# Zeros on TensorE ahead of the first operands, and two early transfers issued by ScalarE

## The chip, the cores and the metric

The kernel runs on one core of a Trainium2 chip. The core has five engines that run their own instruction streams and wait for each other by semaphores: TensorE (PE; its weight loads are listed apart as PEld), VectorE (DVE), ScalarE (ACT), GpSimd (POOL) and SyncE (SP), which here issues nearly all transfers. The transfers themselves run on 16 DMA engines. The metric is the device time of one execution in microseconds; the median of several runs is compared.

## The reference

Two layers on separate inputs, put side by side: attention with 32 heads of 32, and a real-valued Fourier mixing written as products with cosine and sine matrices.

```python
def _A_ref(x, wqkv, wo):                      # x [1, 2048, 1024]
    qkv = ((x @ wqkv).reshape(B, S, 3, 32, 32)).transpose(2, 0, 3, 1, 4)
    q, k, v = qkv[0], qkv[1], qkv[2]
    p = _softmax(jnp.einsum("bhqd,bhkd->bhqk", q, k) * scale, axis=-1)
    o = jnp.einsum("bhqk,bhkd->bhqd", p, v)
    return o.transpose(0, 2, 1, 3).reshape(B, S, D) @ wo

def _B_ref(x, dft_seq_re, dft_seq_im, dft_hid_re, dft_hid_im):
    a = jnp.einsum("bsd,ed->bse", x, dft_hid_re)
    b = jnp.einsum("bsd,ed->bse", x, dft_hid_im)
    return jnp.einsum("ts,bse->bte", dft_seq_re, a) - jnp.einsum("ts,bse->bte", dft_seq_im, b)

out = jnp.concatenate([A_ref(...), B_ref(...)], axis=-1)
```

## The kernel before

The large products are done in Strassen's manner: seven products of sums and differences of blocks in place of eight. Every float32 operand is split in two parts that TensorE takes in one pass each: a rounded high part and the remainder, the low part. A product of two operands is three matmuls: high by high, low by high, high by low. In the trace the high part is a CAST on DVE or an ACTIVATE on ACT (line 442 or 440, in `halves`), the low part a subtraction on DVE or POOL (line 445).

The stage that the change touches is the first one, `qkv`, which makes queries, keys and values. Its first step (`STEPS`, line 549) loads a piece of the query weights, W0, and four tiles of x of 128x512 (`load_x(0, k)`, k from 0 to 3), then runs the first group of twelve matmuls (`group`, line 346; the matmul is line 356): four chunks, three matmuls each, W0 against x0 to x3. The next group takes the second piece of weights, W1, against the same tiles; then come groups with tiles x4 to x7, and then groups with the value weights wv. The results are stored to DRAM (`qk_d`) and loaded again in another layout as `qs` and `ks` for the attention, whose first score matmul is line 1147.

A load is made in `fetch` (line 382): one operand is one transfer of 256 KB, issued on line 404; where a step needs a sum or difference of blocks, a second transfer (line 413) and an addition (line 420) follow. In this stage first operands go to a ring of ten buffers, named `er`, and second operands to a ring of five, named `raw`. A ring is taken in order, and a transfer may start when those who used its buffer before are done.

The program order of all engines is written out by a planner (`Plan`): while the kernel is built it plays the whole of it through with assumed durations. Each operation has an engine, a cost, and some have a second engine that can take it (`other`): the high part may go to DVE or ACT, the low part to POOL or DVE. At each step of its clock the planner goes through ACT, DVE, POOL and SP in this order, and gives a free engine the lowest-ranked operation whose inputs are there (`others`, `choose`). DVE's copies and subtractions share a port with POOL, so the planner runs them one at a time. PE's order has three attention streams (scores S, transposed scores T, values V) and a list of fills, which are the matmuls of all dense products in fixed order; which goes next depends on the planner's clock. On the chip each engine then works through its list strictly in that order.

For a transfer the planner takes 360 KB a microsecond on one pipe, plus 1.6 us to land. When one engine's result is used on another, 0.1 us is added (0.2 after PE), and for some pairs of engines a slack on top:

```python
    LAT = 0.1
    LAT_PE = 0.2
    SLACK = {("SP", "POOL"): 2.0, ("SP", "DVE"): 2.0, ("SP", "PE"): 2.0, ("POOL", "DVE"): 0.7}
    KB_US = 360.0
    LANDING = 1.6
    QUEUE = 1.0
```

The key of the slack is the engine that ran the first operation and the first-named engine of the second. The high part's first-named engine is DVE, the low part's POOL. SP issues its next transfer in the plan no earlier than 1.0 us (`QUEUE`) before the pipe is free; this rule is for SP alone (`begin`, line 204).

PSUM banks for dense products come from two pools of two, `psT` and `psD` (tile `pd`); the first group uses `psT`, the second `pd`.

Of the kernel before, what the change touches and what calls it, by code (L numbers as in the profile page):

```python
# [8 lines left out]
F32 = mybir.dt.float32  # L9
F32R = mybir.dt.float32r  # L10
# [6 lines left out]
P = 128  # L17
# [6 lines left out]
NB = 512  # L24
NPT = 19
NE = 4
PVB = 4
PAIRS = 3
NV = 4
SCALE = float(DH) ** -0.5  # L30
# [30 lines left out]
class Plan:  # L61
# [23 lines left out]
    def op(self, engine, cost, emit, after=(), uses=(), rank=0.0, kb=0, order=None, other=None, lanes=1, two=False):  # L85

        o = Op(engine, cost, emit, rank, kb, other, two)
        o.lanes = lanes  # L90
        seen = set()
        for d in after:
            if d is not None and id(d) not in seen:
                seen.add(id(d))
                self._wait(o, d)
        for u in uses:
            u.append(o)
        if order is not None:
            p, order.first = order.first, o
            if p is not None and not p.begun:  # L100
                p.soon.append(o)
                o.left += 1
        if o.left == 0:
            self._release(o)
        return o
# [104 lines left out]
def kernel(  # L210
# [11 lines left out]
    nc = tc.nc  # L222

    dram = ctx.enter_context(tc.tile_pool(name="dram", bufs=1, space=DRAM))
    const = ctx.enter_context(tc.tile_pool(name="const", bufs=1))
# [21 lines left out]
    def f(ap):  # L247
        return ap.bitcast(F32)
# [19 lines left out]
    qk0 = tc.alloc_tile_pool(name="qk0", bufs=1)  # L268
    QS, KS = [qk0.tile([98, S], F32R, name="qs0")], [qk0.tile([98, S], F32R, name="ks0")]
    nc.gpsimd.memset(f(KS[0])[96:98, :], 1.0)  # L270
    rec = const.tile([P, 2 * NS], F32, name="rec")
    nc.gpsimd.memset(rec, 1.0)

# [14 lines left out]
    psS, psT, psD = (pools[n] for n in ("psS", "psT", "psD"))  # L288
# [19 lines left out]
    ISSUE = 0.46  # L308
# [11 lines left out]
    ADD = 0.68  # L320
    FILL = 3 * (7 * 24 * 4 + 7 * 16 * 4 + 7 * 8 * 16 + 2 * 8 * 4)
    ATT = H * (128 * MM + 16 * PV + 16 / PVB * SWITCH)

    pl = Plan()
    op = pl.op
# [50 lines left out]
    class Kept:  # L376


        def __init__(self, get):
            self.get, self.made, self.users = get, None, []  # L380

    def fetch(shape, terms, store=None, keep=None):

        box = {}
        raws, seconds, tile_of, gate = where[0]
        rank = seq()
        sign, *first = terms[0]
        loaded = len(first) == 2
        if len(terms) == 1 and not loaded:
            return first[0].get, first[0].made, first[0].users  # L390
        if keep is None:
            old, users = raws.take()
        else:

            old, users = gate + keep.users, keep.users

        def dest():
            if "r" not in box:
                box["r"] = tile_of(shape, "raw", len(raws.users)) if keep is None else keep.get()
            return box["r"]  # L400

        last = None
        if loaded:
            last = op("SP", ISSUE, lambda: nc.sync.dma_start(dest(), first[0]), old + first[1] + gate, [users], rank, 256, raws if keep is None else None)
            old = []
        for sign, *term in terms[1:]:
            other = {}
            if len(term) == 2:
                gold, gusers = seconds.take()

                def load(src=term[0], other=other):
                    other["q"] = tile_of(shape, "g", len(seconds.users))
                    nc.sync.dma_start(other["q"], src)

                q = op("SP", ISSUE, load, gold + term[1] + gate, [gusers], rank, 256, seconds)
            else:
                other["k"], q, gusers = term[0], term[0].made, term[0].users

            def add(e, sign=sign, other=other, a=None if last is not None else first[0]):
                (nc.gpsimd if e == "POOL" else nc.vector).tensor_tensor(  # L420
                    out=dest(), in0=dest() if a is None else a.get(), in1=other["q"] if "q" in other else other["k"].get(), op=ALU.add if sign > 0 else ALU.subtract)

            last = op("POOL", SUB, add, old + [first[0].made if last is None else last, q], [users, gusers] + ([first[0].users] if last is None else []),
                      rank, 0, raws if keep is None and last is None else None, other=("DVE", ADD, 20 + rank), two=True)
            old = []
        if keep is not None:
            keep.made = last
        if store is not None:
            store[1].append(op("SP", ISSUE, lambda: nc.sync.dma_start(store[0], dest()), [last], [users], rank, 256))
        return dest, last, users  # L430
# [103 lines left out]
    def qkv():  # L534
# [31 lines left out]
        def load_x(x, k):  # L566
            where[0] = ahead if x < 5 else within
            p = STEPS[x][0]
            XS[x, k] = moving(8 * ((x + 1) % 2) + k, x_terms(p, k, x >= 5), (tx_d[k], tx[k]) if x == 3 else (t1x_d[k], t1x[k]) if x == 2 else None)
# [176 lines left out]
        def qk_group(x, W, b, n):  # L746
            p = STEPS[x][0]
            early = x < 5
            h = FIRST.get(p)
            if p == 1 and n == 0:  # L750
                if early:
                    X[2 * b], X[2 * b + 1] = acc(b)
                else:
                    X[2 * b], X[2 * b + 1] = accs(16 + b - PAIRS)
            group(((chunk(W, c), (XS[x, 4 * n + c], whole)) for c in range(4)), 4,
                  gather(p, 2 * b + n, qk_result(b + 8 * h[0], 2 * h[1] + n, early) if h else None, early, None if b % 2 else SCALE))
# [8 lines left out]
        for x, (p, blocks, v) in enumerate(STEPS[:10]):  # L765
            spare[0] = x < 5
            for i, b in enumerate(blocks):
                where[0] = ahead if x < 5 else within
                W = piece(w_terms(p, lambda i, j: wqk[b + 8 * i][:, 4 * j : 4 * j + 4, :], sq_d[b], sq[b]), (sq_d[b], sq[b]) if p == 6 else None)
                if x == i == 0:  # L770
                    first = W
                    for k in range(4):
                        load_x(0, k)
                    qk_group(x, W, 0, 0)
                    continue
                if x == 0 and i == 1:
                    for k in range(4, 8):
                        load_x(0, k)
                qk_group(x, W, b, 0)
                if x == 0 and i == 1:  # L780
                    qk_group(x, first, 0, 1)
                qk_group(x, W, b, 1)
                if x == 0:
                    if i == 1:
                        for c in range(4):
                            load_v_weight(0, c)
                else:
                    for k in range(8 * i // len(blocks), 8 * (i + 1) // len(blocks)):
                        load_x(x + 1, k)
            for t in range(8 if v else 0):  # L790
                if p == 1 and t % 2 == 0:
                    X[16 + t], X[17 + t] = acc(PAIRS + t // 2)
                v_group(x, t)
                if x == 0:
                    load_x(1, t)
                if t < 4 and x < 4:
                    load_v_weight(x + 1, t)
            where[0] = within
            if x == 4:
                for u in ahead[0].users:  # L800
                    att_gate.extend(u)
            if x == 9:
                for c in range(4):
                    load_v_weight(10, c)
# [446 lines left out]
    def transposed(h):  # L1251
# [4 lines left out]
        for t in range(NS):  # L1256
            for j in range(4):
# [17 lines left out]
                todo.append((t, j, box, e, puse))  # L1275
            if (t + 1) % PVB == 0:
                load, vuse = vts[h]

                def pv(todo=todo, t=t):
                    po["p"] = psD.tile([P, NB], F32, name="pd")  # L1280
                    for k, j, box, _, _ in todo:
                        nc.tensor.matmul(  # L1282
                            po["p"][j * DH : j * DH + DH, :], VT[h][:, k, :], box["t"], start=(k == t + 1 - PVB), stop=(k == t),
                            tile_position=(0, j * DH),
                        )

                v = op("PE", SWITCH + PVB * PV, pv, [load, *(x[3] for x in todo)], [vuse, *(x[4] for x in todo)])
                todo = []

                def gather_o(t=t):  # L1290
                    if t + 1 == PVB:
                        po["o"] = att().tile([P, NB], F32, name="ot", bufs=2)
# [3 lines left out]

                e = op("DVE", EVAC, gather_o, [v] + (oold if t + 1 == PVB else []), [ouse], -1)
                streams["V"].append((v, h, e))
# [42 lines left out]
    while nf < len(fills) or any(place[n] < len(s) for n, s in streams.items()):  # L1341
# [18 lines left out]
        for n, (o, h, k) in heads.items():  # L1360
# [14 lines left out]
            rank = {"V": 0, "T": 1, "S": 0.5 if stock > SFIRST else 1.5}[n]  # L1375
            if n == "S" and "T" in heads and heads["T"][0].left == 0:
# [4 lines left out]
                if lead > 0:  # L1381
                    rank = 2
            ok.append((rank, n))
        fill = None
        if nf < len(fills):
            o, first, left = fills[nf]
# [64 lines left out]
```

## Time and profile before

| what | us |
|---|---|
| median of 3 runs (3045.86 to 3047.76) | 3046.23 |
| the profiled execution | 3044.43 |
| its span, first to last instruction | 3042.6 |
| PE busy in the span | 3009.5 |
| start of the first matmul | 6.10 |
| start of the first score matmul | 72.32 |

A row of the chain or of the timeline has start, duration, engine, line, operation, what is written from what, and a count; in brackets stands how long the engine was idle before and what released it. SPq marks the issue of a transfer by SP, not its flight. A row of waits has: who waited for whom, microseconds in total, times, the longest. A row of windows has the stretch, its length, the busy time of PE, PEld, DVE, ACT and POOL with counts, the granted clock of TensorE as a share of full speed, the busy share of the DMA engines, and GB/s.

### The profile page before, as it was taken

How to read it: one execution, taken by the hardware profiler on the slowest of the kernel's cores; microseconds unless marked ns; L12 is line 12 of the kernel's file. 1: busy time of each engine (PE TensorE's matmuls, PEld its weight loads, DVE VectorE, ACT ScalarE, POOL GpSimd, SP SyncE). 2: the span in 40 equal slices, each digit the busy share in tenths (PEclk: the TensorE clock that was granted, in tenths of full speed). 3: DMA queues.
4: the chain of work that ended last, by engine and by line, in shares of the span. 5: the costliest groups of instructions: out<-in, count | busy, mean ns of one | idle time of the engine just before them, and what ended most of it. 6: DMA issues, size and time to landing. Idle time of an engine off the chain costs nothing.

```text
span 3042.6 us, 45257 instructions
## 1 busy us (share of the span) xinstructions
PE 3009.5 (99%) x14912; PEld 2145.0 (70%) x14912; DVE 2434.8 (80%) x3284; ACT 2298.1 (76%) x4328; POOL 812.6 (27%) x606
## 2 busy tenths in 40 slices
PE   8999999999999999999999999999999999999999
PEld 7887666676676666667766666666677666666887
DVE  7779888778878887787778888888787788887886
ACT  4347888888888888888888888888888788874321
POOL 2313334222412321220111344232111234331232
PEclk9999999999999999999999999999999999999999
DMA  9975567656735544463434675545433567546942
GB/s 336 348 234 186 187 188 234 216 199 227 232 97 175 174 122 157 147 191 113 149 114 129 201 229 185 149 151 182 128 115 100 147 207 237 168 133 222 376 148 98
DMA packets 374777, 557.53 MB, mean 183 GB/s; under 512 B 109424, under 2 KB 109424, under 8 KB 374544
## 3 DMA queue, kind: packets, MB, share of 16 engines
q1 hardware_dynamic: 374544, 554.64, 56.9%
q8 instruction: 120, 1.97, 0.3%
q14 instruction: 113, 0.93, 0.1%
HBM read 401.41 MB, written 152.57 MB: 182 GB/s over the span
## 4 chain that ended last, share of the span: by engine, by line
PE 89%; DVE 5%; DMA 3%; issue 1%; ACT 1%; SPq 0%; POOL 0%; ACTq 0%; DVEq 0%; POOLq 0%
PE pd L356 38%; PE psT L1264 15%; PE psS L1147 15%; PE pd L1282 14%; PE psT L356 7%; DVE negm L1153 2%; ACT psS L1156 1%; DVE slot L442 0%; DVE h L442 0%; DMA raw<-in_wd 0%; DMA raw<-in_ct 0%; DVE raw L420 0%; DMA qk_d<-e 0%; DMA raw<-in_xa 0%; DVE slot L445 0%
## 5 line engine op out<-in xcount | busy, mean ns | idle before, releaser
L1268 ACT ACTIVATE pt<-psT 128x512 f32<-128x512 f32 x2048 | 1169.0, 638 | 350.4 <-PE psT L1264 336.6
L1153 DVE TENSOR_REDUCE negm<-psS 128x1 f32<-128x1024 f32 x1024 | 1237.7, 1220 | 192.5 <-PE psS L1147 187.0
L1156 ACT ACTIVATE psS<-psS,negm 128x1024 f32<-128x1024 f32 x1024 | 1159.8, 1133 | 91.1 <-DVE negm L1153 87.0
L356 PE MATMUL pd<-slot,h 128*128 128x512 f32 x3304 | 1135.6, 394 | 0.0
L1264 PE MATMUL psT<-qs,ks 98*128 98x512 f32 x2048 | 819.3, 403 | 0.8 <-ACT pt L1268 0.8
L356 PEld LDWEIGHTS pd<-slot,h 128*128 128x128 f32 x3304 | 625.2, 189 | 142.5 <-issue 3.4
L356 PE MATMUL pd<-slot,l 128*128 128x512 f32 x1652 | 651.2, 394 | 0.0
L1264 PEld LDWEIGHTS psT<-qs,ks 98*128 98x128 f32 x2048 | 384.2, 189 | 202.3 <-issue 84.7
L1147 PE MATMUL psS<-ks,qs 96*128 96x512 f32 x1552 | 478.2, 397 | 17.6 <-ACT psS L1156 14.5
L1282 PE MATMUL pd<-pt,vt 128*32 128x512 f32 x4096 | 467.5, 597 | 1.5 <-DVE e L641 1.2
L445 POOL TENSOR_TENSOR l<-raw,h 128x512 fp32r<-128x512 f32 x160 | 214.3, 1340 | 944.7 <-DVE h L442 335.0
L420 POOL TENSOR_TENSOR raw<-raw,g 128x512 f32<-128x512 f32 x197 | 260.2, 1325 | 486.4 <-DMA raw<-in_ct 69.8
L356 PEld LDWEIGHTS pd<-slot,l 128*128 128x128 f32 x1652 | 312.9, 189 | 70.0 <-issue 0.8
L1147 PEld LDWEIGHTS psS<-ks,qs 96*128 96x128 f32 x1552 | 290.2, 189 | 92.7 <-ACT psS L1156 27.5
L1282 PEld LDWEIGHTS pd<-pt,vt 128*32 128x32 f32 x4096 | 120.2, 110 | 277.0 <-issue 256.6
L445 POOL TENSOR_TENSOR slot<-raw,slot 128x512 fp32r<-128x512 f32 x135 | 190.7, 1420 | 389.3 <-DVE slot L442 277.5
L1156 ACT ACTIVATION_READ_ACCUMULATOR psS<-psS,negm 128x1 f32 x1024 | 256.6, 251 | 0.0
L1295 DVE TENSOR_TENSOR ot<-ot,pd 128x512 f32<-128x512 f32 x96 | 65.9, 687 | 166.9 <-PE pd L1282 166.9
L356 PE MATMUL pd<-slot,slot 128*128 128x512 f32 x768 | 194.4, 392 | 0.0
L356 PEld LDWEIGHTS pd<-slot,slot 128*128 128x128 f32 x768 | 144.3, 188 | 32.2 <-DVE slot L442 0.3
L1147 PE MATMUL psS<-ks,qx 96*128 96x512 f32 x496 | 151.8, 397 | 2.8 <-ACT psS L1156 2.5
L442 DVE CAST h<-raw 128x512 fp32r<-128x512 f32 x305 | 141.9, 467 | 13.7 <-PE pd L356 12.0
(117 smaller groups left out, 1986.5 us busy)
## 6 DMA issues: line engine op xcount, KB each, us to landing
raw<-in_ct SPq DMA_DIRECT2D x224, 256.0 KB
g<-in_ct SPq DMA_DIRECT2D x128, 256.0 KB
qk_d<-e SPq DMA_DIRECT2D x52, 512.0 KB
qs<-qk_d SPq DMA_DIRECT2D x128, 192.0 KB
ks<-qk_d SPq DMA_DIRECT2D x128, 192.0 KB
raw<-ab_d SPq DMA_DIRECT2D x96, 256.0 KB
c<-u_d SPq DMA_DIRECT2D x88, 256.0 KB
g<-ab_d SPq DMA_DIRECT2D x80, 256.0 KB
```

Of the source, the lines that this page charges most:

```text
L356: nc.tensor.matmul(box["ps"], a[1]((a[0].hi, a[0].lo)[u]()), b[1]((b[0].hi, b[0].lo)[v]()), start=k == 0, stop=k == n - 1)
L420: (nc.gpsimd if e == "POOL" else nc.vector).tensor_tensor(out=dest(), in0=dest() if a is None else a.get(), in1=other["q"] if "q" in other ...
L442: nc.vector.tensor_copy(hi(), raw())
L445: (nc.gpsimd if e == "POOL" else nc.vector).tensor_tensor(out=lo(), in0=raw(), in1=f(hi()), op=ALU.subtract)
L1147: nc.tensor.matmul(p[:, i * NB : i * NB + NB], (qx["t"] if own else QS[h % 2][0:96])[:, qt * P : qt * P + P], KS[h % 2][0:96, c * 1024 + i ...
L1153: nc.vector.tensor_reduce(out=ST["negm"][:, c, qt : qt + 1], in_=box["p"], axis=AX.X, op=ALU.max, negate=True)
L1156: nc.scalar.activation(box["p"], box["p"], AF.Exp, bias=ST["negm"][:, c, qt : qt + 1], accum_out=ST["sums"][:, c, qt : qt + 1])
L1264: nc.tensor.matmul(box["p"], KS[h % 2][0:98, t * P : t * P + P], QS[h % 2][0:98, j * NB : j * NB + NB], start=True, stop=True)
L1268: nc.scalar.activation(box["t"], box["p"], AF.Exp)
L1282: nc.tensor.matmul(po["p"][j * DH : j * DH + DH, :], VT[h][:, k, :], box["t"], start=(k == t + 1 - PVB), stop=(k == t), tile_position=(0, ...
L1295: nc.vector.tensor_tensor(out=po["o"], in0=po["o"], in1=po["p"], op=ALU.add)
```

## The change

A tile of zeros, 128x128, is set by DVE at the start, and TensorE runs 36 matmuls of it by itself into a bank of `psD`, ahead of everything that the planner orders. The result is not used. The planner does not know of these matmuls. The other part: of the first four tiles of x, the first and third (k = 0 and 2) are issued by ACT's queue instead of SP's, and are operations of engine ACT in the plan too.

```diff
+WARM = 36
...
+    zeros = const.tile([P, P], F32R, name="zeros")
+    nc.vector.memset(f(zeros), 0.0)
...
+    ps = psD.tile([P, NB], F32, name="pd")
+    for k in range(WARM):
+        nc.tensor.matmul(ps[:, 0:P], zeros, zeros, start=True, stop=True)
+
     pl = Plan()
...
+    queue = ["SP"]
...
-            last = op("SP", ISSUE, lambda: nc.sync.dma_start(dest(), first[0]), old + first[1] + gate, [users], rank, 256, raws if keep is None else None)
+            q = queue[0]
+            last = op(q, ISSUE, lambda: (nc.scalar if q == "ACT" else nc.sync).dma_start(dest(), first[0]), old + first[1] + gate, [users], rank, 256, raws if keep is None else None)
...
                     for k in range(4):
+                        queue[0] = "SP" if k % 2 else "ACT"
                         load_x(0, k)
+                    queue[0] = "SP"
```

## The prediction

> **What bounds the kernel now.** I read the page's busy times first, then PE's waits over the whole span, then the first 12 us in order of time, then windows of the first 80 us.
>
> ```profile
> span 3042.6 us, 45257 instructions
> PE 3009.5 (99%) x14912; PEld 2145.0 (70%) x14912; DVE 2434.8 (80%) x3284; ACT 2298.1 (76%) x4328; POOL 812.6 (27%) x606
> ...
> DMA  9975567656735544463434675545433567546942
> ...
> PE psS L1147 <- ACT psS L1156: 17.0, 19, 4.0
> PE psS L1147 <- DMA ks<-qk_d: 2.6, 1, 2.6
> ```
>
> TensorE is the bound: 33.1 us of the span are not PE-busy. Of these 6.1 are the wait for the first operand (next rows), 2.6 a wait for the first keys of the attention, 17.0 waits in the attention for ScalarE to free a score bank; the rest is small. So all that the change can touch by its own words is the 6.1 us and how fast the matmuls run right after.
>
> ```profile
> 0.73 1.28 ACT L440 ACT_TABLE_LOAD   x1 [0.73 <-PEq L1444]
> 0.74 0.39 SPq L404 DMA_DIRECT2D er<-in_wqk  x1
> 1.19 1.83 SPq L404 DMA_DIRECT2D er<-in_xa  x4
> 3.32 0.63 ACT L440 ACTIVATE h<-er 128x512 fp32r<-128x512 f32 x1 [1.31 <-DMA er<-in_wqk]
> 3.99 0.69 DVE L445 TENSOR_TENSOR l<-er,h 128x512 fp32r<-128x512 f32 x1 [3.99 <-ACT h L440]
> 5.41 1.32 ACT L440 ACTIVATE slot<-er 128x512 fp32r<-128x512 f32 x2 [1.46 <-DMA er<-in_xa]
> 6.10 0.79 PE L356 MATMUL psT<-slot,h 128*128 128x512 f32 x1 [6.10 <-ACT slot L440]
> 6.16 3.21 SPq L404 DMA_DIRECT2D er<-in_wv  x4
> 7.31 0.63 ACT L440 ACTIVATE slot<-er 128x512 fp32r<-128x512 f32 x1 [0.57 <-DMA er<-in_xa]
> 9.67 0.69 DVE L445 TENSOR_TENSOR l<-er,h 128x512 fp32r<-128x512 f32 x1
> 10.53 0.63 PE L356 MATMUL psT<-slot,l 128*128 128x512 f32 x1
> 10.95 0.43 DVE L442 CAST slot<-er 128x512 fp32r<-128x512 f32 x1
> 10.96 0.63 PE L356 MATMUL psT<-slot,h 128*128 128x512 f32 x1
> 11.38 0.44 PE L356 MATMUL pd<-slot,h 128*128 128x512 f32 x1
> 11.63 0.33 SPq L413 DMA_DIRECT2D raw<-in_xa  x1
> 11.66 0.39 PE L356 MATMUL pd<-slot,l 128*128 128x512 f32 x1
> 11.89 0.39 PE L356 MATMUL pd<-slot,h 128*128 128x512 f32 x1
> ...
> 6.10 5.50 PE psT L356 x12
> ```
>
> The first tile of x lands at 5.41 and is rounded by ScalarE; the first matmul starts at 6.10. Starts then come 0.43 us apart (10.53, 10.96, 11.38) until about 11.5 and 0.23 apart from there (11.66, 11.89). The twelve matmuls of the first group (last row, from the chain of waits) start between 6.10 and the next group's 11.38, 5.28 us; at 0.228 they would take 2.74. **The slow clock costs 2.54 us** here. The windows print a granted clock of 1.00 for this stretch, so the clock must be read from the spacing until the first change is recorded.
>
> ```profile
> 0.00:10.00 10.00, 3.90 (x9) 3.09 (x10) 3.75 (x6) 5.44 (x8) 2.13 (x6) 1.00 0.73 237
> 10.00:20.00 10.00, 10.00 (x41) 7.81 (x40) 8.61 (x12) 7.36 (x14) 2.73 (x2) 1.00 1.01 364
> 60.00:70.00 10.00, 10.00 (x46) 8.29 (x45) 8.40 (x13) 3.79 (x6) 3.03 (x2) 1.00 0.99 350
> ...
> 76.00:77.00 1.00, 1.00 (x5) 0.81 (x4) 1.00 (x2) 0.39 (x1) 0.00 (x0) 0.67 0.54 100
> 77.00:78.00 1.00, 1.00 (x3) 0.73 (x3) 1.00 (x2) 1.00 (x2) 0.68 (x1) 0.50 0.86 266
> 79.00:80.00 1.00, 1.00 (x5) 0.76 (x4) 0.89 (x1) 0.95 (x2) 1.00 (x1) 0.63 1.02 404
> ...
> 75.29 0.96 PE L1147 MATMUL psS<-ks,qs 96*128 96x512 f32 x3 [2.58 <-DMA ks<-qk_d]
> ```
>
> From 10 us on the transfers are full (DMA share 0.96 to 1.02, the column before the last, in every 10 us up to 70), and at 72.7 TensorE runs into them: 2.58 us for keys. The clock then falls to 0.50 for about 3.4 us (0.66 + 2 + 0.74, from the shares of the rows at 76, 77 to 79 and 79), worth 1.7 us. So this stage ends on transfers, not on matmuls.
>
> **The change part by part.** *The zeros.* One DVE memset of 128x128, on an engine idle until 3.99, after the start at 0.73: TensorE can begin near 1.0. No 128-column matmul is in the trace. Below, a column costs what it does in a 512-column one at the slow clock: 0.43/4 = 0.107 us, 36 make 3.9 us, end 4.9, before any operand. Above, each costs as much as a 512-column one: some twelve at 0.43 and 24 at 0.23, 10.7 us, end 11.7; group 1 then ends at 14.4, 3.1 late. I take 0.107, since the 512-column rows at both clocks scale as columns do. Cost nothing, covered by the wait of 6.1; uncovered, it is those 3.1.
>
> The Trainium skill, "TensorE: Matmul & The Clock Gate", Part 1, gives 107 ns for the cold 128-column start, a window of about 3.4 us that runs freely, and full clock after one busy window; this trace agrees with the length (3.4 us at 0.50). The same section speaks against the change: a window of idleness takes the clock away again, and by it a gap behind the zeros would give the 2.54 us back.
>
> *The two issues on ScalarE.* Each costs 0.4 to 0.46 us there, as SP's rows do (0.39; 1.83 for four), ahead of a table load of 1.28: done by about 2.9, before anything lands (3.32). On SP the second tile goes 0.46, the fourth and everything after 0.9 us earlier. When they land is bounded by 3.3 for the first tile (as W now: 0.74 to 3.32) and by 5.4 (no earlier, the engines being shared); for the third by 6.4 and 7.3.
>
> The Trainium skill, "DMA: Bandwidth & Descriptors", "Issuing engines are not separate DMA queues", says that such a move saves only the issue time; by it the third tile lands at 6.4 at best. No row here shows a second issuing engine.
>
> *What the planner makes of it.* This is the larger part. Orders on all engines come from the planner, whose landing time has 2.0 us added where SP issued (SLACK names SP, not ACT). In its clock W0 and the four tiles end at 2.77, 3.48, 4.19, 4.90 and 5.61, changed or not; casts may start at 4.87, 5.58, 6.29, 7.00, 7.71 now, but after the change tile 0 at 3.58 and tile 2 at 5.00. Worked through `choose`: ScalarE casts x0, then W0 (4.87 to 5.47), so x2 at 5.00 goes to DVE. DVE's order becomes x0 low, **x2 cast, x2 low, W0 low** (6.20 to 6.88), x1 low, where now W0 low is first (5.57 to 6.25). On the chip that is a strict queue: W0 low, needed by the second matmul, stands behind the landing of x2. Landing 6.4 to 7.3, plus 0.42 + 0.69 + 0.69, gives 8.2 to 9.1. Eleven matmuls follow: group 1 ends at 10.7 to 11.6 warm, 12.9 to 13.8 cold, against 11.38. Middle of the warm pair: 11.1, a gain of **0.3 us** instead of 2.54. Group 2 needs W1 low (9.67 + 0.69 = 10.36 now), which isn't later than that.
>
> The other consequence: the eleventh transfer (first tile of wv) takes W0's buffer in the ring of ten and may go 0.1 after W0 low: 6.35 now, 6.98 after. SP is free for it at 6.57. Now it goes; after the change it isn't ready, and SP takes what is: the second operand of the third step's x, the `raw<-in_xa` that now stands at 11.63, eighteenth. So wv and all behind it are planned 0.71 us later, one transfer is pulled ahead, and **every later decision of the planner is made with other numbers**: the interleaving of 3 ms is drawn again. That adds no work; it moves holes. A hole, as it is now:
>
> ```profile
> 2409.45 7.43 DMA raw<-ab_d
> ...
> 2416.91 0.69 DVE L420 TENSOR_TENSOR raw<-raw,g 128x512 f32<-128x512 f32 x1 [5.29 <-DMA raw<-ab_d]
> 2420.08 0.73 PE L1147 MATMUL psS<-ks,qs 96*128 96x512 f32 x2 [4.04 <-ACT psS L1156]
> ...
> 2420.00:2430.00 10.00, 9.92 (x51) 4.68 (x52) 6.02 (x9) 6.51 (x13) 3.29 (x3) 0.83 0.53 171
> ```
>
> An add at the head of DVE's queue waits 5.29 us for a transfer that took 7.43; the score maxima behind it are late, ScalarE with them, and TensorE stands for 4.04. Then the clock is 0.83 over 10 us, 3.4 us at half: 1.7 lost. One such hole is **5.7 us**. Whether a new order has more or fewer can't be read from this trace; bounds: minus the 17.0 us of such waits, plus as much again. I take zero.
>
> *Sum.* Against the profiled execution, 3044.43 (span 3042.6 and 1.83 around it): front -0.3, of which the wait for keys at 72.7 can swallow all (it starts earlier if TensorE is earlier; transfers stay full), order 0: 3044.1. The median of the three runs is 3046.23, 1.8 above that execution, so **3045.9** in their terms.
>
> **The rivals.** About 0.2% (6.1 us) is what a measurement of this kernel tells from no change.
>
> *Front kept whole.* If x2 and W0 low come in time and the chain to the keys moves along, 2.54 us of clock and the 0.46 by which the first tile is issued earlier are kept: 3046.2 - 3.0 = 3043.2. For it: part of that chain is PE's evacuations, and DMA is only 0.73 busy in the first 10 us. Against: DVE's order above, and full transfers until 72.7. It too lies within 0.2%.
>
> *The wait takes the zeros' place.* TensorE idles between matmul 1 and 2 (about 6.2 to 8.2 or later); the clock lapses, as after 2.58 us at 72.7. Group 1 ends 1.5 to 2.4 late, at most 3048.6. It belongs to the forecast's own range.
>
> *Fewer holes (faster).* The new order avoids the hole at 2416 and one of half that size: -0.3 - 5.7 - 2 = -8: 3038.2. For it: 17.0 us of waits are there to be avoided. Against: nothing aims at them.
>
> *More holes (slower).* In the attention, 84 to 2800 us, adds land at DVE's head with transfers still out: the planner moves 360 KB a us with 1.6 us landing, while one here took 7.43. Two more such holes: +11.4, 3057.6; from 6.1, just over one hole, it decides. For it: transfers reordered against the ring they wait in, and wv late by plan. Against: DMA is 0.3 to 0.7 busy in most slices of this stretch (the page's row of tenths), and the 19 waits of 17.0 us have a mean of 0.9.
>
> **How the numbers follow.** Forecast (holes about as now) 0.34, front kept whole 0.07, fewer holes 0.27, more holes 0.32. The first two are within 0.2%: 0.41; faster 0.27, slower 0.32. The forecast's own range is 3042 to 3050 (one hole less or less than one more, front -3.0 to +3.1). Holding 8 in 10 needs most of both other cases: 3035 to 3057.
>
> **What would show it.** Right: 36 short matmuls on pd near 1.0 to 5; starts 0.107 apart; ScalarE rounding x before W; on DVE a CAST ahead of the first `l<-er,h`; `raw<-in_xa` as the eleventh transfer, before any wv; a gap of about 2 us behind the first real matmul; a longer wait for ks near 72; the holes of the attention at other places. Wrong: DVE's first four steps as now (then the plan is the same and the time within 3 us), a block of zeros ending after 6, or a first stage ending 3 us earlier at 84. A time outside 0.2% whose difference lies in the first 84 us would refute the argument; one that lies in holes later would confirm the mechanism with its size misjudged.

## The result, and the profile after

| kernel | median of runs, us | ratio to before, 95% interval | profiled span, us |
|---|---|---|---|
| before | 3046.05 (3039.68 to 3048.32) | 1 | 3042.6 |
| after | 3034.43 (3032.89 to 3036.80) | 0.9967 [0.9957, 0.9977] | 3035.0 |

The change is a gain of 0.33%, some 10 us. The forecast was no change. In its terms, where the kernel before takes 3046.2, the ratio gives 3036.2: near the rival "fewer holes", priced at 3038.2, and inside the range of 3035 to 3057. One execution of those in this document (of "two transfers only", below) took 3702.0 us at a granted clock of 0.753; it is left out of its ratio.

The page of the changed kernel, the engines' totals and the DMA row in 40 slices, and then PE's waits (who waited for whom: us in total, times, longest):

```profile
span 3035.0 us, 45328 instructions
PE 3011.9 (99%) x14948; PEld 2150.8 (71%) x14948; DVE 2435.1 (80%) x3287; ACT 2297.6 (76%) x4328; POOL 811.2 (27%) x604
...
DMA  9975567666735545463434676455333567546942
...
PE psS L1160 <- ACT psS L1169: 13.3, 16, 2.4
PE psT L364 <- DVE l L456: 1.4, 1, 1.4
...
PE pd L330 <- DVE zeros L274: 1.1, 1, 1.1
```

PE's idle time falls from 33.1 to 23.1 us. The wait of 6.1 for the first operand and the one of 2.6 for keys are gone, and the waits for a score bank fall from 17.0 to 13.3. But the zeros fill the first wait with work that nobody uses: its 6.1 us is not a gain. The timeline of the start shows what became of it (start, duration, engine, line):

```profile
0.73 0.90 ACTq L415 DMA_DIRECT2D er<-in_xa  x2
1.05 7.75 PEld L330 LDWEIGHTS pd<-zeros 128*128 128x128 f32 x36 [1.05 <-DVE zeros L274]
1.05 7.94 PE L330 MATMUL pd<-zeros 128*128 128x128 f32 x36 [1.05 <-DVE zeros L274]
1.66 1.28 ACT L451 ACT_TABLE_LOAD   x1 [1.66 <-PEq L1457]
5.74 0.63 ACT L451 ACTIVATE slot<-er 128x512 fp32r<-128x512 f32 x1 [2.80 <-DMA er<-in_xa]
6.28 0.61 ACT L451 ACTIVATE h<-er 128x512 fp32r<-128x512 f32 x1
6.78 0.34 SPq L424 DMA_DIRECT2D raw<-in_xa  x1
7.75 0.43 DVE L453 CAST slot<-er 128x512 fp32r<-128x512 f32 x1 [0.65 <-DMA er<-in_xa]
7.81 2.66 SPq L415 DMA_DIRECT2D er<-in_wv  x4
8.21 0.69 DVE L456 TENSOR_TENSOR slot<-er,slot 128x512 fp32r<-128x512 f32 x1
8.79 0.73 PE L364 MATMUL psT<-slot,h 128*128 128x512 f32 x1
8.82 0.69 DVE L456 TENSOR_TENSOR l<-er,h 128x512 fp32r<-128x512 f32 x1
9.56 0.29 PEld L364 LDWEIGHTS psT<-slot,l 128*128 128x128 f32 x1 [0.55 <-DVE l L456]
9.56 0.80 PE L364 MATMUL psT<-slot,l 128*128 128x512 f32 x1
...
13.55 0.39 PE L364 MATMUL psT<-slot,l 128*128 128x512 f32 x1
14.02 0.40 PE L364 MATMUL pd<-slot,h 128*128 128x512 f32 x1
```

The 36 zeros hold TensorE until 8.79, although both operands of the first matmul are rounded by 6.9 (6.28 + 0.61). They take 7.75 / 36 = 0.215 us each, and the slow clock is still there behind them: real matmuls come 0.43 apart until 13.55 and 0.23 from there. The second group starts at 14.02 where it started at 11.38. **The change makes the start 2.64 us later** in these two executions; in another one of the changed kernel, where the clock is recorded as full from 11.68 in place of 13.52, the second group starts at 12.96, 1.6 later.

By the attention that is made good. The first score matmuls in the timeline of the changed kernel, and its clock in the windows (the third column from the end):

```profile
75.66 0.62 PE L364 MATMUL psT<-slot,slot 128*128 128x512 f32 x2
76.12 1.10 PE L1160 MATMUL psS<-ks,qs 96*128 96x512 f32 x4
...
76.00:77.00 1.00, 1.00 (x6) 0.82 (x5) 0.76 (x2) 0.00 (x0) 0.00 (x0) 1.00 1.06 385
77.00:78.00 1.00, 1.00 (x6) 0.79 (x6) 1.00 (x2) 0.46 (x1) 0.00 (x0) 1.00 1.03 399
```

TensorE now comes later than the keys, so it has no wait (2.58 before) and no slow clock (1.7 before). Matched matmul by matmul in the two traces, the changed kernel runs 3.8 us behind from 25 to 70 us, and 0.65 ahead from 84. Its further lead grows later. The same matching, mean offset of PE's matmuls in the two profiled executions, by their time before:

| time before, us | 84 to 200 | 300 to 1000 | 1400 to 1700 | 1800 to 2000 | 2200 to 2400 | 2400 to 2500 | 2600 to the end |
|---|---|---|---|---|---|---|---|
| after minus before, us | -0.65 | -0.3 | -2.6 | -6.2 | -7.8 | -10.5 | -7.6 |

The steps lie at holes that both kernels have and that are smaller after in these two executions. Two of them, in DVE's and PE's timelines, before (the second is the hole of the prediction, whose two rows stand there):

```profile
1289.46 0.43 DVE L442 CAST slot<-raw 128x512 fp32r<-128x512 f32 x1 [4.21 <-DMA raw<-in_wd]
```

and after:

```profile
1285.58 0.43 DVE L453 CAST slot<-raw 128x512 fp32r<-128x512 f32 x1 [1.31 <-DMA raw<-in_wd]
...
2407.53 0.69 DVE L431 TENSOR_TENSOR raw<-raw,g 128x512 f32<-128x512 f32 x1 [3.71 <-DMA raw<-ab_d]
2410.70 0.74 PE L1160 MATMUL psS<-ks,qs 96*128 96x512 f32 x2 [2.45 <-ACT psS L1169]
```

On the add on `ab_d` DVE waits 3.71 us there instead of 5.29, TensorE 2.45 instead of 4.04. No operation was taken out of its way. Matched name by name, TensorE works through the same 14912 matmuls in the same order in both; DVE's list differs up to its 104th instruction, ScalarE's up to about the 77th, GpSimd's up to the 24th, SP's up to about its 134th transfer of 2367. **From about 105 us on every engine works through the same list in both kernels**, and yet they part by 7 us after 1000 us.

The windows of the first 84.1 us, of before and of after (us, busy time of PE, PEld, DVE, ACT and POOL):

```profile
0.00:84.10 84.10, 75.17 (x310) 61.06 (x311) 60.65 (x82) 39.45 (x67) 21.38 (x20) 0.98 0.96 335
```

```profile
0.00:84.10 84.10, 81.58 (x349) 67.91 (x350) 62.34 (x84) 38.94 (x65) 21.37 (x20) 1.00 0.95 333
```

The sum of the difference of the two spans (-7.6): -0.65 up to 84 us. Behind that, PE's idle time falls from 24.2 to 20.6 (the totals of 33.1 and 23.1 less 8.9 and 2.5 in these rows), -3.6; and the clock falls to one half for 3.413 us twice before (2421.29, 2581.72) and once after (2505.24), 1.7 lost each time, -1.7. That is -6.0; the other 1.6 is in no row that I can name. The two executions stand 7.6 apart where the medians stand 11.6 apart: the profile of the changed kernel is of its slowest run.

### The profile page after: what moved, and what is told of

Same layout as the page of the kernel before. It is cut to its first block, busy times and chain, and to the rows that moved or that the text cites. A ratio compares the mean times of both kernels' runs of the same rounds, so it can differ in the third digit from the quotient of the medians.

```text
span 3035.0 us, 45328 instructions
## 1 busy us (share of the span) xinstructions
PE 3011.9 (99%) x14948; PEld 2150.8 (71%) x14948; DVE 2435.1 (80%) x3287; ACT 2297.6 (76%) x4328; POOL 811.2 (27%) x604
## 4 chain that ended last, share of the span: by engine, by line
PE 92%; DVE 4%; DMA 1%; ACT 1%; issue 1%; SPq 0%; POOL 0%; ACTq 0%; DVEq 0%; POOLq 0%
PE pd L364 40%; PE psT L1277 15%; PE psS L1160 15%; PE pd L1295 14%; PE psT L364 7%; DVE negm L1166 2%; ACT psS L1169 1%; DMA g<-in_ct 0%; DVE raw L431 0%; DVE l L456 0%; DVE h L453 0%; DVE slot L453 0%; DVE slot L456 0%; DMA er<-in_xa 0%; SPq L1241 0%
```

## The experiments

A kernel's name stands for its edit against the kernel before, or the changed one where that is said. Ratios are to the kernel before on the same chip. The 105 runs of the kernel before in this study go from 3035.0 to 3052.9 with a mean of 3044.1, so a single profile can be 9 us off its kernel's mean; the ratios carry the verdicts, the profiles the mechanism.

### The two parts, each alone

**Zeros only**: the 36 matmuls of zeros, all orders as before.

```diff
+WARM = 36
...
+    zeros = const.tile([P, P], F32R, name="zeros")
+    nc.vector.memset(f(zeros), 0.0)
...
+    ps = psD.tile([P, NB], F32, name="pd")
+    for k in range(WARM):
+        nc.tensor.matmul(ps[:, 0:P], zeros, zeros, start=True, stop=True)
```

> Before plus the 36 zeros; the planner's order is that of before throughout. Three theories of where the 10 us come from. Order (the new order of the first 135 or so transfers sets everything): no gain, 3046; the zeros end at 8.9 us and hold the first group back by 2.7 us, and the wait for keys at 72.7 us swallows that (2.58 us there now, 0 then), so the attention starts at 75 to 76 us and the later holes stand where they stand in before. Zeros (they are what helps): 3035. Chance (any small change of the program moves the landings of transfers in the attention, up or down): anything from 3034 to 3052, with the holes of the attention at other sizes although the order is the same.

Measured: 0.9995 [0.9984, 1.0006]. The start was that of the changed kernel: zeros until 8.79, the second group at 13.27, then a wait of 1.2 us for keys. The profiled execution was the fastest of its twelve by 5 us (3033.27, the next 3038.59), so its rows are not those of a usual run.

**Two transfers only**: issued by ScalarE and planned so, no zeros.

```diff
+                        queue[0] = "SP" if k % 2 else "ACT"
                         load_x(0, k)
+                    queue[0] = "SP"
```

> Before plus the two transfers on ScalarE's queue, no zeros. Order: as the changed kernel after 84 us, so 3034 to 3036, and up to 2 us less if the front counts (first real matmul at about 6.9 us instead of 8.8). Zeros: 3046. Chance: anything from 3034 to 3052.

Measured: 0.9999 [0.9989, 1.0010]. The timeline of this kernel:

```profile
0.73 0.90 ACTq L407 DMA_DIRECT2D er<-in_xa  x2
5.58 0.63 ACT L443 ACTIVATE slot<-er 128x512 fp32r<-128x512 f32 x1 [2.63 <-DMA er<-in_xa]
6.53 0.33 SPq L416 DMA_DIRECT2D raw<-in_xa  x1
6.78 0.80 PE L356 MATMUL psT<-slot,h 128*128 128x512 f32 x1 [6.78 <-ACT h L443]
7.14 0.43 DVE L445 CAST slot<-er 128x512 fp32r<-128x512 f32 x1 [0.20 <-DMA er<-in_xa]
8.94 0.79 PE L356 MATMUL psT<-slot,l 128*128 128x512 f32 x1 [1.37 <-DVE l L448]
```

The first tile, issued 0.46 us earlier, is there at 5.58 instead of 5.41: nothing is won by the second queue. Over all traces ScalarE starts to round it between 5.41 and 6.26 in the six where ScalarE's queue issued it, and between 5.11 and 5.70 in the eight where SP did. And DVE's new order stands bare here, with no zeros over it: TensorE waits 1.37 us between the first matmul and the second.

**Order only**: the planner's order of the change, but SP issues all transfers, and no zeros.

```diff
-            last = op("SP", ISSUE, lambda: nc.sync.dma_start(dest(), first[0]), ...
+            last = op(q, ISSUE, lambda: nc.sync.dma_start(dest(), first[0]), ...
```

> The planner takes the two transfers as ScalarE's, so all orders are those of the changed kernel, but SP issues them; no zeros. Order: 3034 to 3036 as with ScalarE's queue. If the second queue itself is the cause: 3046. Chance: anything from 3034 to 3052. In every case DVE has the cast of x2 ahead of W0 low and SP has raw as the eleventh transfer.

Measured: 0.9999 [0.9987, 1.0012]. The new order by itself is worth nothing that can be measured. With it falls what the prediction expected of "the interleaving of 3 ms is drawn again".

**Wide zeros**: the order of before, but eleven matmuls of 512 columns (the tile of zeros read four times over) in place of 36 of 128.

```diff
+WARM = 11
...
+    for k in range(WARM):
+        nc.tensor.matmul(ps.rearrange("p (a b) -> p a b", a=4), zeros, zeros.rearrange("p (a b) -> p a b", a=1).broadcast_to([P, 4, P]), start=True, stop=True)
```

> Before plus 11 matmuls of zeros with 512 columns (the tile read four times over) in place of 36 with 128, order of before. If the narrow zeros failed to raise the clock because each waits for its own weight load (0.215 us for 128 columns, half of the array's time), wide ones at 0.43 us keep the array full and end near 5.8 us: the clock rises by 4.7 to 8 us and the first group takes 2.7 to 4 us instead of 5.28. By the theory that the wait for keys at 72.7 us takes the front back, the attention still starts at 74 to 75.3 us and the time is 3044 to 3046; if the front is kept, 3043 or less with the wait for keys at 2.58 us or shorter.

Measured: 0.9978 [0.9968, 0.9988]. These zeros do at the start what the words of the change promise:

```profile
1.05 4.60 PE L330 MATMUL pd<-zeros 128*128 128x512 f32 x11 [1.05 <-DVE zeros L274]
6.39 0.49 PE L364 MATMUL psT<-slot,h 128*128 128x512 f32 x1 [0.73 <-ACT slot L448]
6.72 0.40 PE L364 MATMUL psT<-slot,l 128*128 128x512 f32 x1
7.11 0.73 PE L364 MATMUL psT<-slot,h 128*128 128x512 f32 x2
...
9.33 0.50 PE L364 MATMUL psT<-slot,h 128*128 128x512 f32 x1 [1.02 <-ACT slot L448]
```

They end at 5.65, the clock is recorded as full from 4.96, and real matmuls run at full clock at once. Now the tiles of x are what TensorE waits for (1.02 at 9.33), so group 2 starts at 11.10, only 0.28 before 11.38. In this profile the attention at 84 us is 5.2 us ahead, of 8.9 that its span is shorter. In the profile of "wide zeros again", below, the lead at 84 us is 2.4 of 7.6: a wait of 1.7 for keys and a slow stretch from 73.6 are back there.

### The same again, and both improvements together

**After again** (the changed kernel) and **before again** (the kernel before, run as if it were another), both without an edit, and **wide zeros again**:

> The changed kernel, unaltered. Each half of it alone (e1, e2) and the order alone (e3) gave ratios of 0.9995 to 0.9999. Sampling (its six first runs were drawn low beside six of before that were drawn high; what separates runs is how transfers land in the attention): ratio 0.998 to 1.000, runs scattered over 10 us as before's are. Interaction (both halves together do what neither does alone): 0.9967 again, all runs below 3038.

> The kernel of before, unaltered, against itself: the ratio must be 1 within its interval; its scatter says how far two medians of equal kernels stand apart here. By the scatter of the 35 runs seen (3035 to 3053) a ratio between 0.999 and 1.001.

> Wide zeros in the order of before (e4), unaltered. If its 0.9978 is the front kept (5.2 us at 84 us, 0.17%), 0.998 again, 0.9975 to 0.9988. Sampling: 0.999 to 1.000.

Measured: after again 0.9976 [0.9966, 0.9986], before again 0.9998 [0.9988, 1.0008], wide zeros again 0.9981 [0.9972, 0.9991]. The gain of the change comes again, as 0.24% beside 0.33%; a kernel against itself shows none. But single holes scatter in a kernel that isn't changed. The hole on `ab_d` in before again, and in after again:

```profile
2414.38 0.69 DVE L420 TENSOR_TENSOR raw<-raw,g 128x512 f32<-128x512 f32 x1 [2.81 <-DMA raw<-ab_d]
2417.56 0.73 PE L1147 MATMUL psS<-ks,qs 96*128 96x512 f32 x2 [1.55 <-ACT psS L1156]
```

```profile
2406.51 0.69 DVE L431 TENSOR_TENSOR raw<-raw,g 128x512 f32<-128x512 f32 x1 [2.15 <-DMA raw<-ab_d]
2409.68 0.73 PE L1160 MATMUL psS<-ks,qs 96*128 96x512 f32 x2 [0.89 <-ACT psS L1169]
```

In all fourteen profiles TensorE's wait here is DVE's wait less 1.25 to 1.27 us (from 5.46 and 4.20 in "two transfers only" to 2.15 and 0.89): the add at the head of DVE's queue passes its delay on, and how long the transfer is late differs from run to run. TensorE's wait is 1.55 to 4.20 in the profiles with no zeros or one and 0.89 to 2.80 in those with eleven or more, so at this one hole the two groups overlap.

**Changed kernel with wide zeros**: thirteen of 512 columns in place of its 36.

> The changed kernel with 13 matmuls of zeros of 512 columns in place of 36 with 128: they fill 1.05 to 6.3 us at full use, so the clock is up before the first operand. If a warm front is what counts (e4: attention 5.2 us earlier), the first group ends by 10.7 to 11.6 instead of 13.8, there is no wait for keys, and at 84 us it stands 3 to 5 us ahead of before: ratio 0.9975 to 0.999. If what the clock gains is lost again behind W0 low on DVE (it waits for x2), 0.999 to 1.000.

Measured: 0.9980 [0.9972, 0.9989]. Not faster than the changed kernel, whose zeros do not raise the clock. But the warm clock did not last here:

```profile
1.05 5.52 PE L330 MATMUL pd<-zeros 128*128 128x512 f32 x13 [1.05 <-DVE zeros L274]
6.79 0.49 PE L364 MATMUL psT<-slot,h 128*128 128x512 f32 x1 [0.22 <-ACT h L451]
9.76 0.80 PE L364 MATMUL psT<-slot,l 128*128 128x512 f32 x1 [2.47 <-DVE l L456]
...
13.77 0.39 PE L364 MATMUL pd<-slot,h 128*128 128x512 f32 x1
```

The clock is recorded as full from 5.95. Then W0's low part, behind x2 on DVE, keeps TensorE waiting for 2.47 us between the first matmul and the second; from 9.36 to 12.77 the clock is at half again, and the second group starts at 13.77, 2.4 late. This is what the prediction's rival "the wait takes the zeros' place" describes. So this kernel does not test what a warm first group is worth in the new order.

### What of the zeros it is

**Tile only**: the tile and its memset in the kernel before, no matmul (all tiles behind it move in memory).

> Before plus the tile of zeros and its memset alone: no matmuls, transfers and orders of before. Place (the tile moves every later buffer of the left side of the memory, and that is what changes the landings in the attention): a gain like the changed kernel's, 0.997 to 0.998. Otherwise 0.999 to 1.001.

Measured: 1.0003 [0.9993, 1.0012]. It isn't the placement of buffers. This profile also has a lead at the start that is not kept: matched matmul by matmul it is 3.5 us ahead of before at 84 us, by a shorter wait for keys (1.5) and no slow clock behind it, and its span is 3046.0 against 3042.6.

**One zero** and **half the zeros**: the changed kernel with `WARM = 1` and with `WARM = 18`.

```diff
-WARM = 36
+WARM = 1
```

> The changed kernel with one matmul of zeros in place of 36: same orders, same buffers, same banks; the first real matmul at about 6.9 instead of 8.8 us. If the gain over before comes from the orders and places together, it is all there: 0.996 to 0.998. If the run of 36 zeros counts (interaction with the order): 0.999 to 1.001, as with ScalarE's queue alone. By the front alone (1 to 2 us at 84 us): 0.9994.

> The changed kernel with 18 zeros instead of 36, which end near 5 us, before the operands: nothing is held back, the clock stays low as before. Same orders and places as the changed kernel: 0.996 to 0.998 if those carry the gain, a little below it (by up to 2 us) if the 1.9 us for which zeros held PE up are got back; 0.999 to 1.001 if the level is set by chance for each program.

Measured: one 0.9999 [0.9991, 1.0008], eighteen 0.9987 [0.9978, 0.9997], against 0.9967 and 0.9976 for 36. These kernels differ from the changed one in that number alone: same orders, same queues, same buffers. With one zero the gain is gone, and with eighteen about half or less of it is there; **the gain of the change hangs on its zeros**.

**Zeros only, again**:

> Zeros alone (e1), unaltered. If a program keeps its own level of time in the attention, 0.999 to 1.000 again (0.9995 in e1); if what was seen of e1 and of the changed kernel are draws from one distribution, the two come together: 0.998 to 0.999.

Measured: 0.9987 [0.9976, 0.9998]; with the first, 0.05 to 0.13%. In the order of before the 36 zeros bring less than in the order of the change (0.24 to 0.33%); that the order adds to them is likely, but the intervals of this run and of after again overlap. In the same order of before, wide zeros bring more (0.19 to 0.22%).

All profiles side by side: the page's wait of PE for a score bank, and the time at half clock behind the first group and ahead of the last 30 us (in steps of 3.413 us):

| kernel | zeros | ratio | wait for a score bank, us | half clock, us |
|---|---|---|---|---|
| before; before again | 0 | 1; 0.9998 | 17.0; 18.2 | 10.2; 17.1 |
| tile only | 0 | 1.0003 | 20.7 | 17.1 |
| two transfers only | 0 | 0.9999 | 17.8 | 17.1 |
| order only | 0 | 0.9999 | 16.8 | 17.1 |
| changed, one zero | 1 | 0.9999 | 16.9 | 13.7 |
| changed, half | 18 | 0.9987 | 15.2 | 13.7 |
| zeros only; again | 36 | 0.9995; 0.9987 | 11.0; 14.2 | 3.4; 13.7 |
| wide zeros; again | 11 wide | 0.9978; 0.9981 | 14.8; 14.7 | 6.8; 3.4 |
| changed, wide | 13 wide | 0.9980 | 15.7 | 10.2 |
| after; again | 36 | 0.9967; 0.9976 | 13.3; 13.5 | 3.4; 3.4 |

Every profile without zeros, or with one, waits 16.8 us or more for score banks; every one with eleven or more waits 15.7 or less, and mostly spends less time at half clock too. The contrast is larger here than between the kernels: the six profiles with none or one are of executions that took 3044.4 to 3047.7 us, all above the mean of 3044.1. What holds over all runs is their granted clock: the 156 runs with no zeros or one for which it is recorded have a mean time of 3044.2 and a mean clock of 0.9978, the 83 with eleven or more have 3039.1 and 0.9983. As time lost to the clock this is 6.7 and 5.1 us, so some 1.6 of the 5 us between the groups is clock, and the rest is not. The rows of the two ends, before again, tile only, after again and zeros only:

```profile
PE psS L1147 <- ACT psS L1156: 18.2, 17, 3.7
```

```profile
PE psS L1150 <- ACT psS L1159: 20.7, 19, 3.9
```

```profile
PE psS L1160 <- ACT psS L1169: 13.5, 18, 2.0
```

```profile
PE psS L1155 <- ACT psS L1164: 11.0, 15, 2.1
```

The longest wait differs in the same way (3.7 and 3.9 against 2.0 and 2.1) where their number (17, 19, 18, 15) doesn't. Over all profiles the longest is 2.8 to 4.2 with no zeros or one (15 to 19 waits) and 1.7 to 2.8 with eleven or more (15 to 22 waits): the holes are smaller, not fewer.

Whether a hole costs clock as well depends on where it falls. In each trace the recorded clock changes only at points 3.413 us apart, or a whole number of such steps. In all 40 falls to half clock ahead of the last 30 us, TensorE had been idle for 1.56 to 3.06 us of the 3.413 before the fall, and no such stretch with more than 1.83 us of idle time went without a fall. The wait of 2.45 us in the changed kernel, above, is split by such a point into about 1.4 and 1.0, and the clock stays full; the one of 4.04 before is followed by a fall.

**What stays open** is why work at the start makes holes smaller after 1 and 2.4 ms, in a program whose orders are the same from about 105 us on. What is ruled out as the whole cause: the new order, the second queue and the placement of tiles (each alone 0.9999 to 1.0003), one more matmul on the bank, and a lead at the start (tile only has 3.5 us of it at 84 us and no gain; after has 0.65 and after again 2.7, with the two largest gains; "zeros only, again" is 2.2 behind). The warm clock of the first group can't be the whole cause either, since the narrow zeros of the change leave it slow and bring 0.24 to 0.33%, not less than the wide zeros in the order of before. That it helps there, where the wide bring more than the narrow, is possible and not shown. A guess is that zeros change which transfers meet in the queues at about 100 us, and that this meeting persists; no run here tested it.

## Why the prediction was right or wrong, step by step

**The zeros' price: wrong, and so was their cover.** "I take 0.107, since the 512-column rows at both clocks scale as columns do" measured 0.215. Every zero matmul comes with a weight load of its own, and the block's loads last as long as the block (7.75 of 7.94 us): a load and 128 columns at 0.107 each, one after the other, would make the 0.215; that the two do not overlap is inferred from this sum. For 512 columns the block has no more than the matmuls' own time: eleven take 4.60. So the block ended at 8.8, between the prediction's two ends of 4.9 and 11.7, and not inside the wait of 6.1. The sign for it that the prediction gave, a block of zeros ending after 6, was there.

**The clock: the loss came by another way.** The prediction kept 0.3 us of 2.54, expecting warm zeros and then a gap behind the first matmul that costs DVE's delay. Narrow zeros never raised the clock, in 7.75 us, in any of the four traces with 36 of them. The page that was weighed, the Trainium skill's "TensorE: Matmul & The Clock Gate", Part 1, has full clock after a busy window of about 3.4 us; with 512-column zeros the traces agree (full at 4.96, 5.37 and 5.95, work since 1.05), with 128-column zeros they don't. That they keep the array busy only half of the time, between loads, is the likely reason, and not tested. The second group came 2.64 late, near the bound "those 3.1" in size but with the slow clock in it, which that bound left out. "Changed kernel with wide zeros" shows what the forecast's own chain gives: with zeros that do warm the clock, DVE's delay makes a gap of 2.47 us, the clock is lost at 9.36, and the first group ends at 13.77, at the cold end (12.9 to 13.8) and not at the warm 10.7 to 11.6 from which the 0.3 was taken. A gap of 2.47 us, shorter than the window of about 3.4, was enough.

**DVE's order and SP's eleventh transfer: right, some 0.4 us later than forecast.** ScalarE rounds x0, then W0; DVE casts x2 at 7.75 (its landing was forecast for 6.4 to 7.3), takes its low part and then W0's, which ends at 9.51 (forecast 8.2 to 9.1); `raw<-in_xa` goes ahead of all wv at 6.78. The gap of "about 2 us" is 0.55 in the changed kernel, since the zeros lie over it, and 1.37 in "two transfers only". What the second queue wins: the first tile is rounded from 5.41 before, 5.58 in "two transfers only", 5.74 after, and in no trace with ScalarE's queue before 5.41. The Trainium skill's "DMA: Bandwidth & Descriptors", "Issuing engines are not separate DMA queues", has the issue time as all that can be won; the traces agree that no more was won, and here even the 0.46 us of it came to nothing.

**The wait for keys: wrong sign.** "A longer wait for ks near 72" became none, because TensorE came later, not earlier. What the forecast kept for the whole front, -0.3, measured -0.65 at 84 us, by other terms: +3.8 up to 70 us, less 2.58 of waiting and 1.7 of clock, which leaves -0.5.

**"Every later decision is made with other numbers: the interleaving of 3 ms is drawn again": wrong.** The orders join again by about 105 us, and "order only" has 0.9999. The uncertainty that the prediction hung on this order, of both signs, wasn't there.

**"I take zero" for the holes: the step that failed in the sum.** The term measured -3.6 of idle and -1.7 of clock, some -7 with what no row tells, where the forecast took 0 and the rival "fewer holes" -7.7 (5.7 + 2). The rival had the place (waits for score banks, the hole at 2416 among them) and about the size, but not the cause: no hole went away by a new order, they shrank. The prediction saw one profile and took its holes for a property of the order; the kernel before alone shows the same hole at 1.55 and 4.04. That the time lies within the range is therefore luck as far as the mechanism goes: the low end, 3035, stood for a new order with fewer holes, and no part of the argument let the zeros reach the attention.

## What to carry to other kernels

A warm-up matmul is priced with its weight load: 36 narrow ones took 0.215 us each and left the clock slow, wide ones made it fast in 3.9 to 4.9 us. A warm clock has to be kept as well: a wait of 2.47 us behind the wide ones lost it again. A hole that hangs on a transfer has a size that differs from run to run by as much as the effect that is looked for, so one profile of before does not tell what it costs. A change of 0.2 to 0.3% at such holes can come from an edit that is nowhere near them, so its parts are run alone before the gain is put down to the part it was made for.

## What had not been expected of the hardware

128-column matmuls with their own weights at half clock come 0.215 us apart, and 7.75 us of them did not raise the clock, while 512-column ones raised it at 4.96 to 5.95. The clock falls at points 3.413 us apart, when TensorE was idle for about half of the stretch before (1.56 us or more), so the same hole can cost 1.7 us of clock or none. And zeros in the first 9 us went with a mean time of 3039.1 in place of 3044.2, and in the profiles with waits for score banks of 11.0 to 15.7 us in place of 16.8 to 20.7, with every engine's order the same behind 105 us.
